# Cutting TensorE's warm-up into short matmuls that give way to the first rows of x, and giving the copy of one turned tile to VectorE

## The chip, the cores and the metric

One core of one Trainium2 chip. The metric is the device time of one execution in microseconds (us).

## The reference, cut to what matters

Two independent parts, joined along the last axis: A, a state-space layer, and B, attention over 64 segments of 32 rows with a memory of 8 rows that is handed on.

```python
# part A: x (2048 x 1024)
Bu   = einsum('bld,pd->blp', x, B_bar)          # then a scan over l, then C and Dskip
# part B: x (2048 x 1024), 32 heads of 128
q, k, v = (einsum('btd,dhe->bhte', h, W) for W in (Wq, Wk, Wv))
o = softmax(q k^T * scale, masked) v ; out = einsum('bhte,hed->btd', o, Wo)
```

The kernel begins with part B's values, x Wv. For that it needs x turned (features on the partitions), since the rows arrive untransposed.

## The kernel before: the parts that matter

The opening. x's first four tiles of 128 rows are loaded as they are, turned by TensorE against an identity, and copied from PSUM (the tiles named `ps` in the views, which TensorE's matmuls write) into `xe`. Later tiles of x come through transposing DMAs (`DMA_TRANSPOSE` in the timeline, the first issued at 6.35 us). Wv's first block of 512 columns comes in three pieces.

```python
w0 = b.wl.tile([128, KC, 512], BF16, name="b_wv", bufs=2)
b.load_wv_part(w0, 0, 0, 128, nc.scalar)          # Wv columns 0..127, ACT's DMA queue
for i in range(4):
    b.load_x0(p1, i)                              # x rows of tile i, SP's DMA queue
    if i in (1, 2):
        b.load_wv_part(w0, 0, 128 * i, (256, 512)[i - 1])   # columns 128..255, 256..511

def turn_x0(self, i):
    pt = k.ps("U", (128, 2, KC, 128), BF16)[:, 0, :, :]
    for c in range(KC):                           # KC = 8
        k.PE.transpose(pt[:, c, :], self.x0[i][:, c * 128:(c + 1) * 128], k.ident[:])
    k.copy("vs"[i % 2], self.xe[:, :, 128 * i:128 * i + 128], pt)   # v VectorE, s ScalarE

def v_x(self, hb, q, w):                          # values of one head block, 512 rows
    st = self.next_st()                           # staging buffer, two in turn
    if first:                                     # hb == 0 and q == 0
        ps = [k.ps("P")[:] for _ in range(3)]
        self.turn_x0(0)
        self.turn_x0(1)
        for i, c in ((0, 0), (0, 1), (1, 0), (1, 1)):
            self.v_mm(ps[i], w, i, 128 * c, 128 * c + 128)
        self.turn_x0(2)
        self.v_mm(ps[0], w, 0, 256, 512)
        self.v_mm(ps[1], w, 1, 256, 512)
        self.turn_x0(3)
        # ... cut: tiles 2 and 3 with all 512 columns
    # ... cut: for other blocks 4 x 8 matmuls; four copies PSUM -> st
    Q.dma_start(vx[...], st[...])                 # the staged store, 544 KB, ACT's queue

def next_st(self):
    self.nst += 1
    return self.vst[self.nst % 2]

def warm(k, pool):
    w = pool.tile([128, 512], BF16, name="a_n", bufs=1)
    k.V.memset(w[:], 0.0)
    p = k.ps("R")
    for _ in range(8):
        k.PE.matmul(p[:], w[:, 0:128], w[:], start=True, stop=True)
```

Mind the staging buffer: block 4's copies write the buffer that block 2's store reads, so they wait until that store has landed (at 32.67 us in the trace before; the copy started at 32.75).

## Time and profile before

| | |
|---|---|
| time, 4 runs | 1247.24 us median (1247.18 to 1247.7) |
| TensorE busy | 1234.4 of 1245.6 us |
| first warm-up matmul, first full clock | 1.28 us, 6.33 us |
| x's tiles 0 and 1 landed | 4.23, 5.81 us |
| Wv's columns 256 to 511 landed | 8.91 us |
| second staged store landed | 32.67 us; ScalarE waited for it, TensorE did not |

Landings are the moment when all sixteen updates of the DMA's semaphore were in, and the clock is the first record of the full granted clock; both are read from the trace's events.

In the views, PE is TensorE, PEld its weight loads, DVE VectorE, ACT ScalarE and POOL GpSimd; a q behind a name stands for that engine's sequencer, which issues DMAs; L64 is a line of the kernel.

The page: span, busy time by engine, and the chain that ended last, by engine.

```profile
span 1245.6 us, 20120 instructions
...
PE 1234.4 (99%) x8270; PEld 662.3 (53%) x8342; DVE 668.0 (54%) x1250; ACT 263.5 (21%) x631; POOL 275.8 (22%) x407
...
PE 98%; DMA 1%; issue 0%; ACT 0%; POOL 0%; DVE 0%; SPq 0%; ACTq 0%
```

TensorE is the bound and hardly ever idle (11.2 of 1245.6 us), so only its holes can be won. The opening, as the timeline of TensorE (start, duration, engine, line, operation, tiles, shape, count; in brackets the idle time and what ended it):

```profile
4.24 0.63 PE L64 MATMUL psR<-a_n 128*128 128x512 bf16 x1
4.66 2.02 PE L64 MATMUL psU<-ident,b_xr 128*128 128x128 bf16 x16
6.52 1.06 PE L64 MATMUL psP<-b_wv,b_xe 128*128 128x128 bf16 x16
7.80 1.07 PE L64 MATMUL psP<-b_wv,b_xe 128*128 128x128 bf16 x16 [0.22 <-ACT b_xe L89]
8.70 0.61 PE L64 MATMUL psU<-ident,b_xr 128*128 128x128 bf16 x8
9.15 1.91 PE L64 MATMUL psP<-b_wv,b_xe 128*128 128x256 bf16 x16
```

The last warm-up matmul starts at 4.24, when x's first rows are there; eight more transposes wait for the second rows (from 5.86); tile 1's matmuls wait for ScalarE's copy. The same stretch on the copying engines (timeline of VectorE and ScalarE):

```profile
5.76 0.69 DVE L91 COPY b_xe<-psU 128x1024 bf16<-128x1024 bf16 x1 [2.98 <-PE psU L64]
6.72 1.02 ACT L89 ACTIVATE b_xe<-psU 128x1024 bf16<-128x1024 bf16 x1 [3.90 <-PE psU L64]
```

### The profile page before, as it was taken

The numbers are of one execution on the slowest core, as the hardware profiler recorded it, in microseconds if no ns is written. First come the engines' busy times: TensorE is split into PE (matmuls) and PEld (weight loads), VectorE is DVE, ScalarE is ACT, GpSimd is POOL, SyncE is SP. The second block draws the span as 40 slices with busy tenths as digits, with TensorE's granted clock in tenths as the row PEclk, the third lists the DMA queues.
The fourth block names the chain that finished last, engine by engine and source line by source line (L and its number), as shares of the span: only waits on it lengthen the run. The fifth ranks groups of instructions, "written<-read, shape, count | busy, mean of one in ns | idle before, by whom it ended". The sixth has DMA issues, their size and how long they took to land.

```text
span 1245.6 us, 20120 instructions
## 1 busy us (share of the span) xinstructions
PE 1234.4 (99%) x8270; PEld 662.3 (53%) x8342; DVE 668.0 (54%) x1250; ACT 263.5 (21%) x631; POOL 275.8 (22%) x407
## 2 busy tenths in 40 slices
PE   9999999999999999999999999999999999999998
PEld 5444444444455555556666656555665554446444
DVE  4688899998711124666666666666666641001000
ACT  5344444443310000211112111111211110000000
POOL 4111331212332321322222222222222220000000
PEclk9999999999999999999999999999999999999999
DMA  9965444554898834664454544545473289407000
GB/s 245 272 192 148 131 132 128 144 156 107 241 323 247 251 116 95 192 167 123 95 144 108 144 108 114 138 92 133 96 155 95 61 223 220 110 18 153 17 17 27
DMA packets 316022, 176.83 MB, mean 142 GB/s; under 512 B 138650, under 2 KB 301326, under 8 KB 315926
## 3 DMA queue, kind: packets, MB, share of 16 engines
q1 hardware_dynamic: 293830, 147.95, 48.1%
q10 hardware_dynamic: 21072, 24.38, 5.9%
q0 software_dynamic: 1024, 3.17, 0.7%
q8 instruction: 66, 1.08, 0.4%
q14 instruction: 30, 0.25, 0.1%
HBM read 89.14 MB, written 53.17 MB: 114 GB/s over the span
## 4 chain that ended last, share of the span: by engine, by line
PE 98%; DMA 1%; issue 0%; ACT 0%; POOL 0%; DVE 0%; SPq 0%; ACTq 0%
PE psP L64 82%; PE psU L64 9%; PE psS L64 3%; PE psO L64 2%; PE psR L64 2%; DMA wo<-in_B_Wo_dram 1%; DMA b_xr<-in_B_x_dram 0%; ACT b_xe L89 0%; POOL b_m L644 0%; DVE b_ost L91 0%; SPq L64 0%; ACT b_e L641 0%; ACTq L89 0%
## 5 line engine op out<-in xcount | busy, mean ns | idle before, releaser
L64 PE MATMUL psP<-b_xe,b_wq 128*128 128x480 bf16 (+1 forms) x1280 | 247.7, 343 | 0.1
L64 PE MATMUL psP<-b_xe,b_wk 128*128 128x480 bf16 (+1 forms) x1280 | 247.7, 343 | 0.0
L64 PE MATMUL psP<-b_wv,b_xe 128*128 128x512 bf16 (+2 forms) x1033 | 223.4, 372 | 1.0 <-ACT b_xe L89 0.2
L644 POOL TENSOR_TENSOR b_m<-b_e,maskB 99x396 bf16<-99x396 bf16 x160 | 139.8, 874 | 334.0 <-ACT b_e L641 334.0
L641 ACT ACTIVATE b_e<-psS 99x396 bf16<-99x396 f32 x176 | 88.2, 501 | 532.2 <-PE psS L64 527.9
L64 PEld LDWEIGHTS <-b_wk 128*128 128x128 bf16 x1280 | 119.4, 98 | 94.2
L64 PEld LDWEIGHTS <-b_wq 128*128 128x128 bf16 x1280 | 118.7, 98 | 87.7
L64 PEld LDWEIGHTS <-b_xe 128*128 128x128 bf16 x1056 | 101.8, 98 | 119.1 <-ACT b_xe L89 0.4
L91 DVE CAST b_k<-psP 128x480 bf16<-128x480 f32 (+1 forms) x192 | 97.5, 529 | 101.1 <-PE psP L64 101.1
L91 DVE CAST b_q<-psP 128x480 bf16<-128x480 f32 (+1 forms) x192 | 97.5, 529 | 93.0 <-PE psP L64 91.4
L64 PEld LDWEIGHTS <-b_ol 128*128 128x128 bf16 x864 | 84.3, 98 | 94.4
L64 PE MATMUL psU<-a_xT,a_bt 128*128 128x512 bf16 x493 | 113.9, 379 | 1.1
L64 PE MATMUL psP<-t,a_hl 128*128 128x512 bf16 x496 | 112.1, 379 | 0.8
L91 DVE CAST b_ost<-psP 128x512 bf16<-128x512 f32 (+1 forms) x17 | 11.5, 676 | 183.4 <-PE psP L64 182.4
L64 PE MATMUL psP<-wo,b_ol 128*128 128x512 bf16 (+1 forms) x440 | 91.9, 364 | 0.4
L64 PE MATMUL psP<-t,b_ol 128*128 128x512 bf16 x408 | 91.7, 379 | 0.4
L280 POOL TENSOR_SCALAR a_tt<-a_pr,a_tabf 128x1 f32<-128x1 f32 x48 | 34.1, 709 | 243.5 <-DVE a_pr L275 243.5
L89 ACT ACTIVATE b_vst<-psP 128x512 bf16<-128x512 f32 x126 | 72.0, 589 | 71.0 <-PE psP L64 65.0
L661 DVE TENSOR_TENSOR b_ob<-psO,b_accR 99x384 bf16<-99x384 f32 x160 | 85.9, 553 | 2.0
L267 DVE TENSOR_TENSOR a_pr<-psU,a_tabf 128x2048 f32<-128x2048 f32 x32 | 73.0, 2282 | 15.7 <-PE psU L64 14.0
L64 PEld LDWEIGHTS <-a_bt 128*128 128x128 bf16 x512 | 49.2, 98 | 57.6
L64 PEld LDWEIGHTS <-a_hl 128*128 128x128 bf16 x512 | 49.1, 98 | 56.7
(200 smaller groups left out, 963.8 us busy)
## 6 DMA issues: line engine op xcount, KB each, us to landing
b_v<-b_vx SPq DMA_DIRECT2D x16, 1122.0 KB
b_wv<-in_B_Wv_dram SPq DMA_DIRECT2D x16, 1024.0 KB
b_on<-b_ob SPq DMA_DIRECT2D x15, 960.0 KB
b_vx<-b_vst ACTq DMA_DIRECT2D x24, 544.0 KB
a_hs<-a_h SPq DMA_DIRECT2D x32, 256.0 KB
b_wog<-in_B_Wo_dram SPq DMA_DIRECT2D x4, 2048.0 KB
b_wq<-in_B_Wq_dram SPq DMA_DIRECT2D x16, 512.0 KB
b_wk<-in_B_Wk_dram SPq DMA_DIRECT2D x16, 512.0 KB
```

Source lines behind the costliest of these rows:

```text
L64: r = f(*a, **kw)
L89: self.S.activation(out, in_, ACT.Copy)
L91: self.V.tensor_copy(out, in_)
L267: V.tensor_tensor(pr[:], u[:].unsqueeze(1).to_broadcast([128, 2, 2, TB]), view(t3, [[TB + 1, 2], [TB + 1, 2], [1, TB]]), ALU.mult)
L280: G.tensor_scalar(tt[:, j:j + 1], w[:, j, TB - 1:TB], t3[:, 1, TB:TB + 1], None, ALU.mult)
L641: k.S.activation(e[:], s[0:GW, :, :, 0:GW], ACT.Exp, scale=float(E) ** -0.5, accum_out=self.accE[0:GW, i:i + 1])
L644: k.G.tensor_tensor(m[0:GW, 0:4 * GP].rearrange("p (a b q) -> p a b q", a=2, b=2)[:, :, :, 0:GW], e[:], mask[0:GW, :, :].unsqueeze(2).to_b ...
L661: V.tensor_tensor(self.ob[:, b0:b0 + n, :], o[0:GW, 0:n, 0:E], r.unsqueeze(2).to_broadcast([GW, n, E]), ALU.mult)
```

## The change

Its intent: hand TensorE to x's first rows as soon as they land, keep it busy with six more warm-up matmuls while the second rows are on their way, and have the faster copier (VectorE, 0.69 us against 1.02) copy both tiles that are waited for.

```diff
-        k.copy("vs"[i % 2], self.xe[:, :, 128 * i:128 * i + 128], pt)
+        k.copy("vs"[i // 2], self.xe[:, :, 128 * i:128 * i + 128], pt)
...
             self.turn_x0(0)
+            k.warm(6)
             self.turn_x0(1)
...
-    w = pool.tile([128, 512], BF16, name="a_n", bufs=1)
+    w = pool.tile([128, 128], BF16, name="a_n", bufs=1)
     k.V.memset(w[:], 0.0)
     p = k.ps("R")
-    for _ in range(8):
-        k.PE.matmul(p[:], w[:, 0:128], w[:], start=True, stop=True)
+
+    def more(n):
+        for _ in range(n):
+            k.PE.matmul(p[:, 0:128], w[:], w[:], start=True, stop=True)
+    more(24)
+    k.warm = more
```

## The prediction

> **What bounds the kernel now.** TensorE. The profile page has PE busy for 1234.4 of 1245.6 us, and 98% of the chain that ended last is PE. Start-to-start distances in the timeline leave only two real holes in PE's opening, and none of note between 12 and 1000 us. So whatever the change moves, it can only win or lose in the first 12 us; behind that the kernel should shift as a block.
>
> **The opening, from the timeline and the DMA landings.** Eight 128x512 warm-up matmuls start at 1.28 us, 0.427 us apart, and give way at 4.66. x's first rows have landed at 4.23, so they wait about 0.4 us behind the warm-up. Their 8 transposes go 0.107 us apart until 5.5. Then PE waits (hole 1, 0.34 us) for x's second rows, landed at 5.81, turned from 5.86. At 6.33 the granted clock rises and spacing falls to 0.056 us. Tile 0's 16 matmuls go from 6.52 to 7.41. Then PE waits (hole 2, 7.41 to 7.80, 0.39 us) for ScalarE's copy of tile 1 (6.72 to 7.74, 1.02 us). VectorE's copy of tile 0 took 0.69 us. The next weights (Wv columns 256 to 511) landed at 8.91; their matmuls began at 9.15.
>
> **What the change does.**
> 1. Shorter warm-up: 24 x 0.107 = 2.6 us (estimate), from about 1.1 us (smaller memset) to about 3.7. Tile 0 is turned from 4.28 instead of 4.66 and copied by about 6.05 instead of 6.45. But nothing used that earlier copy: tile 0's matmuls stand behind tile 1's turn, which waits for the landing at 5.81. Direct gain: 0.
> 2. Six more warm-up matmuls, 5.13 to 5.77: they fill hole 1, which is DMA-bound and stays. Cost 0, at most 0.05 us.
> 3. VectorE instead of ScalarE for tile 1: copy 6.72 to 7.41, matmuls from 7.46 instead of 7.80: 0.34 us gained.
> 4. Given back: the turn of tile 2 then ends at about 8.81, before the weights of 8.91 are there. PE waits about 0.1 us and goes on at 8.96 instead of 9.15. What stays is about 0.19 us.
> 5. ScalarE copies tile 2 instead (about 9.07 to 10.09): needed only at about 11.2, so free.
>
> Behind that, Wv's next block (landed 12.27, used at 15.2) and the later x tiles (slack of several us) can take the shift.
>
> **The clock.** [...] The trace agrees with both spacings (0.427 and 0.107 us cold, 0.056 warm) and with one release, 5.05 us after the first matmul. The new warm-up leaves a hole of about 0.55 us (3.7 to 4.25) and fills one of 0.34. [...] An earlier release (8%) would win a few tenths.
>
> **Predicted.** 1247.27 - 0.19 = 1247.1 us; range 1246.3 to 1248.0 (the three runs before spread over 0.5 us). Chances: faster by over 2% 0.00, within 2% 0.99, slower by over 2% 0.01.
>
> **Right if** tile 1's copy is a VectorE copy of about 0.69 us and its matmuls start near 7.46; the matmuls on columns 256 to 511 start right on a DMA landing near 8.9; the clock is granted near 6.3; PE's order and busy time beyond 15 us are unchanged.
>
> **Wrong if** the release of the clock moves, VectorE's cast of the index table gets in front of tile 1's copy, the landings move, or the reordering of instructions in later stages (attention, output) changes and moves the time by a microsecond or more.

Two sentences of its part on the clock are cut, since no trace of this case shows what they said of the release; the first is what the trace is said to agree with, and the second gave 12% to a later release. The forecast's sum has no term from them and stands: 1247.27 - 0.19 = 1247.1 us.

## More of the kernel before

ScalarE near 30 us (timeline): it issues the third staged store and then copies block 4's results from PSUM.

```profile
30.20 0.37 ACTq L494 DMA_DIRECT2D b_vx<-b_vst  x1
32.75 1.08 ACT L89 ACTIVATE b_vst<-psP 128x512 bf16<-128x512 f32 x2 [1.97 <-PE psP L64]
```

The view puts the start at 32.75 down to TensorE, but the second store's semaphore filled at 32.67, so the landing ended this wait: ScalarE already waited here, and TensorE did not notice.

TensorE runs through the values without a break from 15.20 to 36.12 us (timeline):

```profile
15.20 20.92 PE L64 MATMUL psP<-b_wv,b_xe 128*128 128x512 bf16 x94
```

And the DMA traffic by stretch (columns: the stretch, its length, busy time of PE, PEld, DVE, ACT and POOL with their counts, granted clock, DMA share, GB/s):

```profile
32.00:33.00 1.00, 1.00 (x7) 0.45 (x5) 0.00 (x0) 0.25 (x1) 0.00 (x0) 1.00 1.26 286
33.00:34.00 1.00, 1.00 (x6) 0.43 (x5) 0.00 (x0) 1.00 (x3) 0.00 (x0) 1.00 1.27 290
...
37.00:38.00 1.00, 1.00 (x6) 0.49 (x5) 0.55 (x1) 0.00 (x0) 0.00 (x0) 1.00 2.85 183
38.00:39.00 1.00, 1.00 (x7) 0.41 (x6) 0.00 (x0) 0.00 (x0) 0.00 (x0) 1.00 0.07 7
```

Between 38 and 39 us the DMAs moved 7 GB/s where they moved 286 and 290 between 32 and 34.

## The result and the profile after

1248.31 us median of 4 runs (1248.77, 1248.22, 1248.39 and 1247.09), against 1247.24 before. The ratio is 1.0006, interval 0.9989 to 1.0024: the same within noise. A ratio here is the mean time of one kernel's runs over that of the other's of the same rounds, so it is not quite the ratio of the medians. Still, three of four runs are a microsecond longer, and the profiled one (1248.77) shows where.

The page after:

```profile
span 1247.0 us, 20164 instructions
...
PE 97%; DMA 2%; ACT 1%; issue 0%; POOL 0%; DVE 0%; ACTq 0%
PE psP L64 81%; PE psU L64 9%; PE psS L64 3%; PE psO L64 2%; PE psR L64 2%; DMA b_vx<-b_vst 1%; DMA wo<-in_B_Wo_dram 1%; DMA b_xr<-in_B_x_dram 0%; ACT b_vst L89 0%; ACT L187 0%; POOL b_m L645 0%; ACT a_fr L236 0%; ACT a_k L233 0%; ACT a_k L229 0%; ACT a_tabf L231 0%
```

A new link stands in the chain: the store `b_vx<-b_vst`. The opening after (timeline of TensorE, and VectorE's copy of tile 1):

```profile
1.08 2.74 PE L64 MATMUL psR<-a_n 128*128 128x128 bf16 x24 [1.08 <-DVE hpb L105]
4.17 1.04 PE L64 MATMUL psU<-ident,b_xr 128*128 128x128 bf16 x8 [0.36 <-DMA b_xr<-in_B_x_dram]
5.00 0.85 PE L64 MATMUL psR<-a_n 128*128 128x128 bf16 x6
5.73 1.04 PE L64 MATMUL psU<-ident,b_xr 128*128 128x128 bf16 x8
6.56 2.21 PE L64 MATMUL psP<-b_wv,b_xe 128*128 128x128 bf16 x32
8.61 0.61 PE L64 MATMUL psU<-ident,b_xr 128*128 128x128 bf16 x8
9.15 1.91 PE L64 MATMUL psP<-b_wv,b_xe 128*128 128x256 bf16 x16
```

```profile
6.80 0.69 DVE L91 COPY b_xe<-psU 128x1024 bf16<-128x1024 bf16 x1 [0.53 <-PE psU L64]
```

Everything is as the change means it: rows turned on landing, the fill behind them, all 32 matmuls of tiles 0 and 1 without a wait. And at 9.15 us the kernel stands where it stood before, because the next weights landed at 9.11 (8.91 before). Nothing is won or lost in the opening of this run. (The clock was released at 7.10 instead of 6.33, so tile 0's matmuls ran longer, 0.107 us apart up to the release and 0.056 behind it, and tile 1's began at 7.71, only 0.09 us earlier than before.)

The microsecond comes at 33 us (timeline of ScalarE, then of TensorE, then the DMA traffic by stretch):

```profile
30.20 0.37 ACTq L495 DMA_DIRECT2D b_vx<-b_vst  x1
34.65 1.08 ACT L89 ACTIVATE b_vst<-psP 128x512 bf16<-128x512 f32 x2 [3.87 <-DMA b_vx<-b_vst]
```

```profile
29.70 4.70 PE L64 MATMUL psP<-b_wv,b_xe 128*128 128x512 bf16 x20
35.30 1.89 PE L64 MATMUL psP<-b_wv,b_xe 128*128 128x512 bf16 x8 [0.91 <-ACT b_vst L89]
```

```profile
32.00:33.00 1.00, 1.00 (x7) 0.46 (x5) 0.00 (x0) 0.00 (x0) 0.00 (x0) 1.00 1.27 341
33.00:34.00 1.00, 1.00 (x6) 0.43 (x5) 0.00 (x0) 0.00 (x0) 0.00 (x0) 1.00 1.82 12
34.00:35.00 1.00, 0.39 (x2) 0.10 (x1) 0.00 (x0) 0.35 (x1) 0.00 (x0) 1.00 0.76 168
```

The DMAs stand nearly still between 33 and 34 us (12 GB/s). The second staged store lands at 34.57 instead of 32.67, ScalarE's copies wait for it (3.87 us idle), and TensorE stops for 0.91 us, until ScalarE has copied. From there on VectorE's instructions run 1.06 us behind those of before, and from 493 us 1.36 us, without a change to the end. The order of instructions on every engine is the same in both kernels, except for the warm-up itself and the copies of tiles 1 and 2.

The hole in the traffic after 33 us is the one that stood at 38 us before. In both traces a packet of 16384 bytes on the queue that the page calls "q8 instruction" starts just before it: at 37.13 us before, at 32.58 after. I call such a packet a fetch. The queue's name says instructions; that they are TensorE's is an inference: each trace has 66 of these packets, and between the start of one and of the next TensorE began 253 instructions on average before and 254 after (from the trace's events, weight loads and matmuls counted singly), some 16700 in all, while the engine with the next most, VectorE, has 1406 in the whole trace.

So theory C, at this point only argued: the 44 added instructions move TensorE's fetches; each fetch is followed by a hole of a microsecond and more in all DMA traffic; moved to 33 us, the hole meets the one store that the program waits for. It was written down after the first four experiments. Those were expected with two theories: chance (A, later also called E), and the change itself (B), through the number of its instructions or through the timing of the warm-up and the clock. A later rival (D) is that any added short matmul costs time, in proportion.

### The profile page after: what moved, and what is told of

Same layout as the page of the kernel before. It is cut to its first block, busy times and chain, and to the rows that moved or that the text cites. A ratio compares the mean times of both kernels' runs of the same rounds, so it can differ in the third digit from the quotient of the medians.

```text
span 1247.0 us, 20164 instructions
## 1 busy us (share of the span) xinstructions
PE 1235.0 (99%) x8292; PEld 664.7 (53%) x8364; DVE 667.9 (54%) x1250; ACT 263.4 (21%) x631; POOL 275.8 (22%) x407
## 4 chain that ended last, share of the span: by engine, by line
PE 97%; DMA 2%; ACT 1%; issue 0%; POOL 0%; DVE 0%; ACTq 0%
PE psP L64 81%; PE psU L64 9%; PE psS L64 3%; PE psO L64 2%; PE psR L64 2%; DMA b_vx<-b_vst 1%; DMA wo<-in_B_Wo_dram 1%; DMA b_xr<-in_B_x_dram 0%; ACT b_vst L89 0%; ACT L187 0%; POOL b_m L645 0%; ACT a_fr L236 0%; ACT a_k L233 0%; ACT a_k L229 0%; ACT a_tabf L231 0%
## 5 line engine op out<-in xcount | busy, mean ns | idle before, releaser
L91 DVE CAST b_ost<-psP 128x512 bf16<-128x512 f32 (+1 forms) x17 | 11.5, 676 | 183.4 <-PE psP L64 182.4
```

The costliest lines, as they stand in the source:

```text
L91: self.V.tensor_copy(out, in_)
```

## The experiments

One table first. "Extra" counts TensorE's instructions beyond the kernel before. "Fetch" is the start of the 16 KB packet near 35 us, "hole" the stretch behind it with under 48 GB/s on the two hardware_dynamic queues together (in quarters of a us), "store" the landing of the second staged store, "lost" how much TensorE fell behind there (the shift of VectorE's instructions against the kernel before, at 45 us minus at 27 us). These five and the clock's release are from the one profiled run. "Mean" is that of 5 runs (4 for the first two), "against" its difference from the kernel before in the same rounds.

| kernel | extra | clock | fetch | hole | store | lost | mean us | against | runs over 1248.0 |
|---|---|---|---|---|---|---|---|---|---|
| before | 0 | 6.33 | 37.13 | 37.75-39.0 | 32.67 | - | 1247.34 | - | 0 of 4 |
| after | 44 | 7.10 | 32.58 | 33.0-34.25 | 34.57 | 1.07 | 1248.12 | +0.78 | 3 of 4 |
| after_again | 44 | 4.91 | 32.73 | 33.25-34.5 | 32.71 | 0 | 1247.87 | +0.36 | 3 of 5 |
| copy_only | 0 | 4.46 | 36.83 | 37.5-38.75 | 31.50 | 0 | 1247.31 | -0.20 | 0 of 5 |
| warm_only | 44 | 4.09 | 32.28 | 32.5-34.0 | 34.33 | 1.27 | 1248.15 | +0.64 | 4 of 5 |
| few_long | 0 | 4.91 | 36.80 | 37.5-38.75 | 32.24 | 0 | 1247.24 | -0.27 | 0 of 5 |
| plus22 | 22 | 4.37 | 38.33 | 39.0-40.25 | 33.11 | 0 | 1247.24 | -0.46 | 0 of 5 |
| plus88 | 88 | 6.61 | 31.90 | 32.5-33.75 | 33.88 | 0.54 | 1248.25 | +0.55 | 3 of 5 |
| vst3 | 44 | 5.24 | 31.61 | 32.25-33.25 | 33.59 | 0 | 1247.34 | -0.37 | 0 of 5 |
| wv_first | 0 | 7.05 | 37.49 | 38.25-39.25 | 32.82 | 0 | 1247.26 | -0.44 | 0 of 5 |
| before44 | 44 | 6.92 | 32.25 | 32.75-34.0 | 34.24 | 0.82 | 1247.70 | +0.28 | 3 of 5 |
| no_fill | -4 | 9.26 | 37.26 | 37.75-39.0 | 32.12 | 0 | 1248.02 | +0.60 | 3 of 5 |
| combined | 0 | 6.46 | 37.79 | 38.75-39.5, broken once | 32.76 | 0 | 1246.95 | -0.46 | 0 of 5 |
| combined_2 | 0 | 5.45 | 37.28 | 38.25-39.0 | 33.35 | 0 | 1247.32 | -0.19 | 0 of 5 |

The kernel before itself had 3 of 40 runs over 1248.0. That line at 1248.0 was drawn after seeing the first runs; from plus22 on it stood in expectations. The means before were 1247.51 (first four experiments), 1247.70 (next four), 1247.41 and 1247.51. Kernels are compared only within the same rounds.

### after_again: does it come back?

The changed kernel, unaltered.

> The changed kernel again, unaltered, to learn whether its three slower runs of four (about 1248.2 to 1248.8 us) come back. Theory A (chance: the landing of the third staged store at 33 us varies from run to run, whatever the kernel): its times mix with those of the kernel before, both between 1247.1 and 1248.8, ratio 1.000 within 0.0003. Theory B (the change itself moves DMA work later): again most runs about 1 us slower, ratio 1.0006 to 1.0009, and in the profile ScalarE again waits for the landing of a b_vx store until about 34.5 us.

Three of five runs were over 1248.0 again; the ratio was 1.0004, below the 1.0006 to 1.0009 that theory B asked for. The profiled run was one of the short ones (1247.1), and it shows why a kernel with the same program can be quick: the store landed at 32.71 us, half a microsecond before the hole began at 33.25. Landing and hole run a race, and some executions win it. Chance alone (A) falls with the counts below.

### copy_only and warm_only: which half?

copy_only is the kernel before with this line of the change alone; warm_only is the changed kernel with this line undone.

```diff
-        k.copy("vs"[i % 2], self.xe[:, :, 128 * i:128 * i + 128], pt)
+        k.copy("vs"[i // 2], self.xe[:, :, 128 * i:128 * i + 128], pt)
```

> Only the copy of turned tile 1 goes to VectorE; the warm-up stays as it was (8 long matmuls, same instruction count on TensorE). Both theories: tile 1's copy 0.69 us instead of 1.02, its matmuls from about 7.46 instead of 7.80, then a wait for Wv's columns 256 to 511 (landing near 8.9), so TensorE is about 0.2 us ahead at 11.5 us. Theory A: total like before, less 0.0 to 0.2 us. Theory B, in the form that the added warm-up instructions are to blame: no run above 1247.8 us, ratio 0.9998 to 1.0000.

> Only the warm-up is changed (24 short matmuls, 6 more behind the first turn; 44 more instructions on TensorE); tile 1 stays with ScalarE. Theory A: like before within 0.3 us. Theory B (the warm-up's instructions are to blame): most runs about 1 us slower, ratio 1.0006 to 1.0010, with TensorE's instruction fetches at about 13.4, 32.6 and 59.5 us as in the changed kernel instead of 14.6 and 37.1.

The loss went with the warm-up: warm_only had 4 of 5 runs over 1248.0, and TensorE waited 1.1 us for `b_vst` (view of the waits: total, times, longest); copy_only had neither.

```profile
PE psP L64 <- ACT b_vst L89: 1.1, 1, 1.1
```

The copy alone removed the wait for ScalarE, as meant, but TensorE was not 0.2 us ahead at 11.5: it was 0.1 behind, because Wv's columns 256 to 511 landed at 9.24. Of the eleven kernels of the table with the original order of loads, seven start their first matmul on these columns 0.03 to 0.05 us after that landing (8.69 on 8.65, 8.74 on 8.70, 9.15 on 9.11, 9.29 on 9.24 among them). The other four (before, plus88, before44, no_fill) come later than the landing, and all four had the clock released after 6.3 us (as had the changed kernel, which did meet the landing). So a faster copy can win only what the landing leaves.

### few_long: the same warm-up in as few instructions as before

The whole change, with both parts of the warm-up made of long matmuls.

```diff
-    w = pool.tile([128, 128], BF16, name="a_n", bufs=1)
+    w = pool.tile([128, 512], BF16, name="a_n", bufs=1)
...
-    more(24)
+    more(6, 512)        # 6 matmuls of 512 columns
...
-            k.warm(6)
+            k.warm(2, 384)
```

> The whole change, with the same warm-up time in as few instructions as before: 6 matmuls of 128x512, then 2 of 128x384 behind the first turn (about 2.6 and 0.64 us, as the 24 and the 6). Theory B in the form of instruction count: times like before (about 1247.2), fetches back at 14.6 and 37.1 us. Theory B in the form of warm-up timing or clock release: still about 1 us slower like the changed kernel. Theory A: like all the others.

No run over 1247.7, mean 0.27 us below the kernel before, the fetches back at 14.1 and 36.8 us. The hand-over, the fill and the copy are all there; only the number of instructions and the shape of the warm-up matmuls differ from the changed kernel. In the profiled run TensorE was 0.45 us ahead from 12 us on, and gave back 0.22 us near 493 us, where it waits for the first load of `b_v`.

### plus22 and plus88: is the loss proportional to the added instructions?

few_long with the first part cut finer: `more(17, 180)`, and `more(50, 61)` on 32-column weights.

> As few_long, but the first part of the warm-up is cut into 17 matmuls of 128x180 (same time, 22 instructions more than before). Theory C (TensorE's 16 KB instruction fetch stops the SP queue's data for about 1 us; what counts is whether the fetch falls before the second staged store has landed at about 32.5 us): the fetch moves from 36.8 to about 34.5 us, behind the landing; no run above 1248.0 us, median 1247.1 to 1247.5. Rival D (any added short warm-up matmuls cost time, in proportion): about half of the changed kernel's loss, median near 1247.7.

> As few_long, but the first part of the warm-up is 50 matmuls of 61 columns on 32-column weights (about the same time, 88 instructions more than before). Theory C: the fetch moves to about 27.5 us, between the store's issue (25.1) and its landing, so the landing comes 1 to 2 us late and ScalarE waits for it: median 1248 to 1249. Rival D: twice the loss, about 1249. Rival E (chance): like before.

It is not proportional: with 22 more the mean was 0.46 us below the kernel before, with 88 more 0.55 above, and 44 more lost about the same as 88 (rival D falls). The fetch of plus22 came behind the store's landing, as theory C asked, but at 38.3 us and not at 34.5. That of plus88 came at 31.9, not at 27.5. So where a fetch lands does not follow from counting instructions in the way I counted; what places it is open.

### before44: nothing but the count

The kernel before, with its last two warm-up matmuls replaced by 24 tiny ones of about the same time. No early hand-over, no other copy.

```diff
-    for _ in range(8):
+    for _ in range(6):
         k.PE.matmul(p[:], w[:, 0:128], w[:], start=True, stop=True)
+    for _ in range(24):
+        k.PE.matmul(p[0:32, 0:32], w[:, 0:32], w[:, 0:32], start=True, stop=True)
```

> The kernel before, with its copies and without the early hand-over; only the last two of its 8 warm-up matmuls are replaced by 24 tiny ones (32 columns on 32-column weights), which are 44 instructions more on TensorE. Theory C (instruction count alone): TensorE's fetch comes near 32.5 us instead of 37.1, a hole of about 1.2 us in the data moved follows it, the second staged store lands near 34 us or later, and the times are like warm_only's (most runs 1248.0 to 1248.8, mean 0.4 to 0.8 us above the kernel before). If the early hand-over or the form of the warm-up is to blame: like the kernel before.

Three of five runs were over 1248.0 (1248.06 to 1248.38), the other two under 1247.0; the mean lies 0.28 us above, less than the 0.4 to 0.8 expected. The profiled run shows the same picture as the changed kernel (traffic by stretch):

```profile
32.00:33.00 1.00, 1.00 (x6) 0.47 (x5) 0.00 (x0) 0.00 (x0) 0.00 (x0) 1.00 2.53 227
33.00:34.00 1.00, 1.00 (x7) 0.47 (x5) 0.00 (x0) 0.00 (x0) 0.00 (x0) 1.00 0.06 6
34.00:35.00 1.00, 0.34 (x3) 0.06 (x2) 0.00 (x0) 0.68 (x2) 0.00 (x0) 1.00 1.16 262
```

6 GB/s in the microsecond after the fetch, then TensorE idle. Taken together, the kernels with 44 more instructions and two staging buffers had 13 of 19 runs over 1248.0, those with at most 22 more (copy_only, few_long, plus22, wv_first) 0 of 20. (no_fill, slow for another reason, is left out; the kernel before had 3 of 40.) In all 14 profiles of the table, each of the two 16 KB fetches between 11 and 45 us was followed within 1.1 us by such a hole: 24 of the 28 holes lasted 1.0 to 1.5 us, the other four 0.5 to 0.75. (Holes of this kind also stand near 28 us, behind an 8 KB packet on the other instruction queue, at 28.41 us before and 27.38 after, in most of the traces. Elsewhere between 11 and 45 us only shorter ones do.) In the changed kernel the store's last data packet ended by 32.57 us; fifteen of its sixteen completion signals came only behind the hole, at 34.50 and later.

### vst3: take the wait away, leave the hole

The changed kernel with a third staging buffer for block 3, so that block 4 writes the buffer of block 1, whose store landed near 20 us.

```diff
+        self.vs3 = tmp.tile([128, 4, 4, EW], BF16, name="b_vst2", bufs=1)
...
         self.nst += 1
-        return self.vst[self.nst % 2]
+        if self.nst == 3:
+            return self.vs3
+        return self.vst[(self.nst - (self.nst > 3)) % 2]
```

> The changed kernel with its 44 added instructions, but a third staging buffer for the third block, so that ScalarE's copy of the fourth block no longer waits for the second store. Theory C, and the claim that this wait carries the loss: the fetch still comes at about 32.6 us and the store still lands near 34.5 in most runs, but ScalarE's copies start near 31 us, TensorE does not wait, and no run is above 1248.0 us; median 1247.0 to 1247.5. If the loss lies elsewhere (later x tiles delayed too): still 1248 and more.

ScalarE in the profiled run (timeline), and the DMA traffic:

```profile
30.83 0.60 ACT L89 ACTIVATE b_vst<-psP 128x512 bf16<-128x512 f32 x1 [0.20 <-PE psP L64]
32.56 0.60 ACT L89 ACTIVATE b_vst<-psP 128x512 bf16<-128x512 f32 x1 [1.13 <-PE psP L64]
```

```profile
32.00:33.00 1.00, 1.00 (x6) 0.42 (x5) 0.00 (x0) 0.44 (x1) 0.00 (x0) 1.00 1.84 21
```

The hole is there (21 GB/s), the store lands late (33.59 us), and nobody waits: ScalarE copies from 30.83, as TensorE delivers. No run over 1247.6, mean 0.37 us below the kernel before.

The profiles also allow a sum. Take the store's lateness as its landing less 32.67 us, plus TensorE's lead over the kernel before at 27 us (0.01, 0.46, 0.15 and 0.10 us in the four below), since a kernel that is ahead needs the buffer earlier. The four profiles that lost time had a lateness of 1.9 (after), 2.1 (warm_only), 1.4 (plus88) and 1.7 us (before44), and lateness less loss was 0.83 to 0.84 us in all four. With two buffers and at most 0.71 us (plus22) nothing was lost; with the third buffer 1.06 (vst3) and 1.30 us (combined_2) cost nothing either. (In the kernel before, the store's data ended by 32.07 us, so 0.5 us of the lateness of 1.9 in the changed kernel, whose data ended by 32.57, arose before the hole; by this sum that part alone would have cost nothing.) So in every profile with two buffers ScalarE waits for this store (its copy starts 0.08 to 0.09 us after the landing), TensorE can bear 0.84 us of lateness, and what comes on top costs it one for one.

With that the cause is settled to this point: added instructions move the fetch and the hole behind it, and the hole costs through this one wait. That the fetch itself makes the hole is not shown apart from their always coming together.

### no_fill: is the fill behind tile 0 needed?

few_long without `k.warm(2, 384)`.

> few_long without the two warm-up matmuls behind the turn of tile 0. If these do what the change wants of them (they keep TensorE busy so that the clock is released): the release comes later or is spread more widely, and the mean rises by some tenths of a us. [...] like few_long (within 0.2 us of it relative to the kernel before), release somewhere between 4 and 7.2 us.

The first of the two: three of five runs were over 1248.3, the mean 0.60 us above the kernel before; in the profiled run the fetch was in its harmless place. That run's opening (timeline of TensorE):

```profile
1.28 2.74 PE L64 MATMUL psR<-a_n 128*128 128x512 bf16 x6 [1.28 <-DVE hpb L105]
4.07 1.04 PE L64 MATMUL psU<-ident,b_xr 128*128 128x128 bf16 x8
5.63 1.04 PE L64 MATMUL psU<-ident,b_xr 128*128 128x128 bf16 x8 [0.53 <-DMA b_xr<-in_B_x_dram]
6.46 3.29 PE L64 MATMUL psP<-b_wv,b_xe 128*128 128x128 bf16 x32
9.59 0.61 PE L64 MATMUL psU<-ident,b_xr 128*128 128x128 bf16 x8
```

The 32 matmuls of tiles 0 and 1 take 3.29 us instead of 2.21: the clock was released only at 9.26 us, and by 15 us the kernel was 0.88 us behind. In the other 13 profiles the release lay between 4.09 and 7.10 us, a spread of 3.0. The stretch of full clock lasted 1235.62 us in no_fill, 1242.45 in warm_only and 1239.04 in the twelve others, lengths that lie 3.42 and 3.41 us apart.

What decides the release is not shown. What went with the late one is: between the turns of tiles 0 and 1 TensorE stood idle for 0.53 us in no_fill; in few_long two warm-up matmuls start there, at 4.82, its idle time is 0.21, and the clock was released at 4.91. So the matmuls behind tile 0 win no time directly but probably keep the hand-over from costing the clock. few_long, which has them, had no run over 1248.0, but on another chip, and only one run of no_fill was profiled; and copy_only, which has no such matmuls either and waited 0.46 us at the same place, was released at 4.46.

### wv_first and combined: a better version?

The landing of Wv's third piece ends the opening. wv_first is few_long with that piece loaded before x's third rows and used before tile 2 is turned:

```diff
-                if i in (1, 2):
-                    b.load_wv_part(w0, 0, 128 * i, (256, 512)[i - 1])
+                if i == 1:
+                    b.load_wv_part(w0, 0, 128, 256)
+                    b.load_wv_part(w0, 0, 256, 512)
...
-            self.turn_x0(2)
             self.v_mm(ps[0], w, 0, 256, 512)
+            self.turn_x0(2)
             self.v_mm(ps[1], w, 1, 256, 512)
```

> As few_long, but Wv's columns 256 to 511 are loaded before x's third rows, and tile 0's matmuls on them come before tile 2 is turned. If the landing of those weights is what ended the opening in all kernels (8.65 to 9.24 us): it lands about 0.7 us earlier (near 8.0), their matmuls start by about 8.1 to 8.4, TensorE is 0.4 to 0.6 us further ahead at 15 us than in few_long; of the total 0 to 0.5 us remain (1246.6 to 1247.1), since the waits for the staged store at 33 us and for the value load at 490 us keep wall-clock time.

The piece landed at 8.07 us and no matmul of the opening waited for it; but in the profiled run the clock was released at 7.05, so TensorE got to these matmuls only at 8.56 and was not further ahead than few_long. The mean is 0.44 us below the kernel before; the total fell in the expected place only in part (1246.75 to 1247.61).

combined is wv_first with vst3's third buffer.

> few_long with the third staging buffer and with the weights loaded before x's third rows: the three changes that the runs speak for. If the waits found so far are all there is: TensorE ahead of the kernel before by 0.3 to 0.9 us at 15 us (depending on the release of the clock), no wait for a staged store at 33 us, about 0.2 us given back near 490 us; mean about 0.4 to 0.6 us below the kernel before of the same rounds, no run above 1247.7 us.

> The combined kernel a second time, with its own runs of the kernel before, to see whether the gain of 0.46 us stands: mean 0.2 to 0.7 us below the kernel before, and no run above 1247.7 us (the two slow states, late staged store and missed release of the clock, should both stay away). If the first call was luck: within 0.2 us of the kernel before.

In the first all five runs (1246.75 to 1247.12) lay below the fastest of nine runs of the kernel before (1247.22), the mean 0.46 us below. In the second the mean was 0.19 below, at the edge of what was expected, with runs up to 1247.59. So it was no slower than the kernel before, and none of its ten runs was a long one; a gain of 0.2 to 0.5 us is likely but not clear of noise.

## Why the prediction was right or wrong

The forecast of "within 2%" was right, and the ratio of 1.0006 is not clear of noise. It says little for the mechanism, as 2% are 25 us and the opening that was argued about is 12 us long. The predicted 1247.1 us was not met: the median was 1248.31, 0.3 above the top of the range.

1. *Shorter warm-up, direct gain 0.* Right: tile 0 was turned from 4.17, and its copy (done 5.94) was not waited for.
2. *Six more matmuls, cost 0.* Right in time. But I called them only a filler of a DMA-bound hole, and did not see that they probably guard against the later release that I had given 12%: in no_fill, without them, the mean was 0.60 us above the kernel before, and in its profiled run the clock was released only at 9.26 us.
3. *VectorE's copy wins 0.34 us.* The mechanism was right (0.69 us, no wait left), the size was off: in the profiled run tile 1's matmuls began at 7.71 instead of 7.80, as the clock came later (7.10 instead of 6.33) and tile 0's matmuls ended later.
4. *Given back to the landing of Wv's third piece, 0.19 left.* The mechanism was right and shown in several traces; what is left is whatever that landing gives: 0 us in the profiled run (9.11), 0.41 in after_again (8.70), 0.1 lost in copy_only (9.24).
5. *ScalarE's copy of tile 2 is free.* Right: 9.25 to 10.27, needed at 11.5.
6. *"Behind that the kernel should shift as a block."* This is the step that failed. I looked for slack in the loads that the opening feeds, and not at what the added instructions themselves do. They moved TensorE's instruction fetch from 37.1 to 32.6 us, and the hole behind it (12 GB/s) held up a store on which ScalarE waits; TensorE lost 1.06 us there. The trace before showed ScalarE waiting 1.97 us for this very store, with 0.84 us of slack for TensorE behind that wait; I did not ask what would make it later. Another 0.30 us went near 493 us, which is not shown to come from the fetch.
7. *The clock: a later release 12%*. Neither profile of the changed kernel has a release later than 7.10 us, which fits the fill; the profiled run of no_fill had one (9.26). Still, two of my own conditions for "wrong" held in the profiled run: the release moved (7.10 instead of 6.33), and so did the landing of Wv's third piece (9.11 instead of 8.91).

Left open: why the traffic stops behind a fetch, what sets its exact place, and what made 3 of 40 runs of the kernel before long. The 0.2 to 0.3 us that several kernels lose near 493 us, at the first load of `b_v`, were seen and not pursued.

## What to carry to other kernels

Instructions that cost no time on their engine can still cost through where they move a fetch (44 of them moved one from 37.13 to 32.58 us, and TensorE lost 1.06 us there), so prefer few long filler matmuls to many short ones, and compare where the fetches fall relative to any DMA that somebody waits for. A wait of another engine for a transfer that only the slack of the bounding engine hides (here ScalarE's 1.97 us, with 0.84 us of slack for TensorE) can be exposed by the next harmless edit; look for those before predicting that a kernel shifts as a block. When the clock's release varies by microseconds from run to run (4.91 and 7.10 us in two profiles of the changed kernel), keep the engine filled across the hand-overs (in the one profile of no_fill, without the fill, the release came at 9.26), and judge changes of the opening by several executions, not by one profile.
